# First FFN product of the last three pieces by seven block products, with the buffers and weight passes that go with it

## The chip, the cores and the metric

One NeuronCore of a Trainium2 chip runs the whole program. The metric is the device time of one execution in microseconds. Inputs and outputs lie in HBM; the two FFN weights arrive as 64-bit floats, the rest as 32-bit floats.

## The reference

```python
def _attn_ref(q, k, v):                      # 8 batches, 8 heads, 576 rows, 64 columns
    scores = np.matmul(q, k.transpose(0, 1, 3, 2)) / np.sqrt(64)
    # a row of block i (blocks of 64 rows) sees the columns of blocks 0..i
    scores = np.where(mask, scores, -1e9)
    attn = np.exp(scores - scores.max(-1, keepdims=True))
    attn = attn / (attn.sum(-1, keepdims=True) + 1e-09)
    return np.matmul(attn, v)

def _moe_ref(x, w_in, w_out):                # x: 4608 x 512, w_in: 512 x 2048, w_out: 2048 x 512
    h = x @ w_in
    g = h * np.clip(h + 3.0, 0.0, 6.0) / 6.0
    return g @ w_out
```

The attention output, with its heads side by side, is `x`.

## The kernel before

**Number format.** A 32-bit value is carried as two 16-bit halves, `hi` and `lo = value - hi`, after division by a power of two. A product of two such values is three 16-bit matmuls: hi by hi, hi by lo, lo by hi. Each matmul is issued as a pair, one for each half of 64 output partitions.

**Attention.** 32 slots (8 batches, 4 pairs of heads each). A slot loads q and k, splits and transposes them by DMA (`qk_prep`, tile `qkT`, two buffers), makes the masked scores in three row groups (`s_group`, PSUM tile `s`), takes row maxima on DVE, exponentials on ACT, splits the probabilities (`ph`, `phl`), transposes them by DMA (`pT`; the third group's tile has the tag `pT2`, two buffers) and multiplies by v (`pv_group`, PSUM `pv`, into the x buffers `xb`). Batch 0 runs in 32 bits without the split.

**FFN.** The 4608 rows form 13 pieces, numbered 0 to 12; all have 384 rows but pieces 1 and 3, which have 192. Piece `pc` keeps its x in `xb[pc % 4]`. A piece has 16 steps `f` of 128 hidden columns. `ffn1(pc, f)` makes `h` (PSUM tag `h`, two buffers) with 12 pairs of matmuls of 384 columns, then the nonlinearity: ACT writes `r` (relu6 inner part), DVE multiplies, then `g` is split (hi on ACT or DVE, lo on DVE; tag `g`, four buffers). `ffn2(pc, f)` adds `g` times `wout` into three PSUM tiles `o0` to `o2`, one buffer each, with 9 pairs of 512 columns; it runs `LAG = 3` steps behind. After step 15 the three tiles are scaled into `osb` (tag `stage`, four buffers, which `r` uses too) and stored.

**Weights.** 32 half chunks are loaded (tag `raw` and others), turned from 64 to 32 bits, bounded (`w_max`: an ACT pass with absolute value and sum for each half, then a small DVE reduction) and split (`w_split`: hi on ACT, DVE or POOL, lo on DVE). This happens beside batch 0's attention and piece 0.

**Order.** The program does not run in the order in which it is written. `Recorder` collects every engine instruction with a key (its planned time: tables `AT` for the slots, `FT` for the pieces, and constants for the rest), then `schedule` simulates the five engines with a table of costs, takes at each moment the ready instruction with the smallest key, and emits that order. All engine instructions therefore have one line, L491. A tile gets its buffer only when the written order allows it: an instruction that starts a tile waits until no earlier written, unfinished tiles fill all buffers of its tag:

```python
            if i > head and need[tag][head:i].max() >= bufs[tag]:
                full[tag] = i
                return 1e18
```

`step` writes FFN steps as soon as the attention rows of their piece are written; `ffn_step` decides how far `ffn2` follows.

Of the kernel before, what the change touches and what calls it, by code (L numbers as in the profile page):

```python
# [8 lines left out]
F16 = mybir.dt.float16  # L9
# [8 lines left out]
P = 128  # L18
# [7 lines left out]
U = 1.592  # L26
AS = (6.899, 12.918, 18.225, 24.115)
AL = 17.759
PV0 = 2.584
TA, TR, PR = 2.701, 5.502, 1.15  # L30
QR = 2.616
PVA, PVB = 1.013, 0.991
# [6 lines left out]
EVP = 4  # L39
PRO = True  # L40
MEM = 0

NMIN = 64
QL = -3.431
VL = -2.484
W0, WD = 16.803, 2.29
S0, SD = 55.334, 4.109
M0, MD = 36.221, 7.195
RT = (29.488, 39.58, 49.409, 59.423)
RS, RL, VL1 = 2.209, 24.843, 24.11  # L50
VM0, VMX = 49.529, 0.186
# [3 lines left out]
QP = 0.558  # L55
VP = 0.387
BLK = 64
# [24 lines left out]
ADV = {("tensor", "a"): 99.24}  # L82


class Recorder:
# [12 lines left out]
    BIAS = {"vector": 250.0, "gpsimd": 500.0}  # L98
# [3 lines left out]
    def __init__(self, nc):  # L102
        self.nc = nc
        self.ops = []
        self.key = 0.0
        self.cls = ""
        self.joint = None
        self.adv = ADV
        for n in self.NAMES:
# [6 lines left out]
    def box(a):  # L116
        sz = mybir.dt.size(a.dtype)
# [58 lines left out]
    def add(self, ways):  # L176
# [318 lines left out]
def kernel(  # L495
# [51 lines left out]
    ffp = ctx.enter_context(tc.tile_pool(name="ff", bufs=3))  # L547
    ps_s = ctx.enter_context(tc.tile_pool(name="ps_s", bufs=3, space=bass.MemoryType.PSUM))
# [12 lines left out]
    def pow2_scale(mx, n, nm, to=None, exact=False):  # L561
# [8 lines left out]
        if exact:  # L570
            pt_ = ps_s.tile([P, 512], F32, tag="s", name=f"mt_{nm}")
            nc.joint = "mt", nm
            for h in range(2):
                wide = mx[:, h % n:h % n + 1].to_broadcast([P, BLK])
                nc.tensor.matmul(pt_[h * BLK:(h + 1) * BLK, :P], wide, ident, start=True, stop=True)
            nc.joint = None
            dg = sm.tile([P, n + 1], F32, tag=f"dg{n}", name=f"dg_{nm}")
            nc.vector.tensor_reduce(dg[:, n:], pt_[:, :P], axis=AX.X, op=ALU.max)
            nc.vector.tensor_scalar_mul(dg[:, :n], ident[:, :(n - 1) * BLK + 1:BLK], dg[:, n:])
            mx = dg[:, :n]  # L580
        ps = ps_s.tile([P, 512], F32, tag="s", name=f"mb_{nm}")
        nc.joint = "mb", nm
        for h in range(2):
            nc.tensor.matmul(ps[h * BLK:(h + 1) * BLK, :n], ones[:, :BLK], mx, start=True, stop=True)
        nc.joint = None
        nc.vector.tensor_scalar_max(am, ps[:, :n], TINY)
# [90 lines left out]

    def w_max(c):

        acc = sm.tile([P, 2, 2], F32, tag="wacc", bufs=2, name=f"wacc{c}")  # L680
# [66 lines left out]
    def v_max(n):  # L747
# [8 lines left out]
        if hp == NPAIR - 1:  # L756
            m1 = sm.tile([P, 1], F32, tag="vm1", name=f"vm1_{b}")
            nc.vector.tensor_reduce(m1, vmax[b], axis=AX.X, op=ALU.max)
            vscale[b] = pow2_scale(m1, 1, f"v{b}", exact=True)
# [13 lines left out]
    def h_scale(b):  # L773

        if b not in hs:
            t = sm.tile([P, NCH], F32, tag="sh", bufs=3, name=f"sh{b}")
# [3 lines left out]
            nc.vector.tensor_scalar_mul(t, t, C_H)  # L780
            hs[b] = t
        return hs[b]
# [374 lines left out]
    def pv_group(n, g):  # L1157
# [57 lines left out]
    acc = {}  # L1215

# [29 lines left out]
    def ffn1_(pc, f):  # L1246
        if pc == 0:
            return ffn1_f32(f)
        x, w, fc = xb[pc % 4], width(pc), f * P % NH
# [52 lines left out]
    def ffn2_(pc, f):  # L1302
# [34 lines left out]
        for t, a in enumerate(acc.pop(pc)):  # L1337
            n, half = min(w - t * P, P), w - t * P < P
            o = ffp.tile([P, DM], F32, tag="stage", bufs=NST_B, name=f"osb{pc}_{t}")
            oc = o[:, :DM // 2] if half else o  # L1340
            ac = a[:, :DM // 2] if half else a
            nc.scaled(oc, ac, so[:, t:t + 1] if pc else 1.0 / 6.0, "AV")
            rows = out[row + t * P:row + t * P + n]
# [86 lines left out]
    for n in range(NPAIR):  # L1430
        t = RT[n]
        at(t - QR, qk_load32_rest, n, lead=RL - QR)
        at(t - QR, qk_prep32, n, 1)
# [94 lines left out]
```

## Time and profile before

| | |
|---|---|
| median of three runs | 985.25 us (983.32 to 985.38) |
| profiled execution, its own time | 982.83 us |
| its span | 981.0 us |
| granted TensorE clock, mean | 0.999 |
| busy: PE, DVE, ACT, POOL | 964.2, 756.4, 696.5, 28.3 us |

Times in the rows are microseconds from the start of the span unless marked ns. PE is the matmul engine, PEld its weight loads, which overlap the matmuls. A group's mean is the duration of one instruction; consecutive instructions of one engine overlap somewhat, so the distance between two starts is the better price where a timeline shows it.

### The profile page before, as it was taken

Reading aid. Unit: us, or ns where it says so; the run is one execution under the profiler, and the core shown is the slowest. Engines: PE = TensorE matmul, PEld = TensorE weight load, DVE = VectorE, ACT = ScalarE, POOL = GpSimd, SP = SyncE. Lnnn points to the kernel's source line nnn. Section 1 sums busy time; section 2 is a strip of 40 time slices with the busy share of each in tenths; the row PEclk is TensorE's granted clock in tenths of the full one; section 3 lists DMA queues with packets and bytes.
Section 4 is the critical chain, followed back from the end, with each engine's and each line's share of the span. In section 5 each row is a group of like instructions: output and inputs, shape, how many; then the busy total and the mean of one; then the engine's idle time right before and its main releaser. Section 6 shows DMA issues by size and latency. Waiting matters only on the chain.

```text
span 981.0 us, 29087 instructions
## 1 busy us (share of the span) xinstructions
PE 964.2 (98%) x11754; PEld 722.9 (74%) x11754; DVE 756.4 (77%) x2081; ACT 696.5 (71%) x1840; POOL 28.3 (3%) x109
## 2 busy tenths in 40 slices
PE   8999999999999999999999999999999999999998
PEld 6655447877778867777777677777777777777776
DVE  6889998999989999999999898899886432332331
ACT  6899789778778888888878788787775433333332
POOL 3012000000000000000000000000000000000000
PEclk9999999999999999999999999999999999999999
DMA  6966689899898899898899898786664200000000
GB/s 141 277 204 223 159 154 178 169 183 189 155 173 148 149 175 157 170 162 148 161 186 177 151 188 156 132 164 131 108 133 77 36 34 1 1 33 1 34 2 33
DMA packets 414199, 128.91 MB, mean 131 GB/s; under 512 B 403184, under 2 KB 403440, under 8 KB 414064
## 3 DMA queue, kind: packets, MB, share of 16 engines
q1 hardware_dynamic: 414064, 127.05, 66.5%
q8 instruction: 92, 1.51, 0.6%
q14 instruction: 43, 0.35, 0.1%
HBM read 45.09 MB, written 9.44 MB: 56 GB/s over the span
## 4 chain that ended last, share of the span: by engine, by line
PE 58%; DVE 6%; DMA 2%; ACT 1%; issue 1%; DVEq 0%; ACTq 0%
PE o L491 25%; PE h L491 25%; PE s L491 4%; PE pv L491 4%; DMA pT<-ph 2%; DVE st L491 1%; DVE phl L491 1%; DVE ph L491 1%; DVE r L491 1%; DVE g L491 1%; DVE qks L491 1%; DVE vhl L491 0%; ACT p L491 0%; DVE x L491 0%; ACT r L491 0%
## 5 line engine op out<-in xcount | busy, mean ns | idle before, releaser
L491 PE MATMUL h<-x,win 128*64 128x384 f16 (+3 forms) x4790 | 440.7, 319 | 4.4 <-DVE r L491 4.4
L491 PE MATMUL o<-wout,g 128*64 128x512 f16 (+2 forms) x3424 | 432.3, 383 | 0.0
L491 PEld LDWEIGHTS <-win 128*64 128x64 f16 x4608 | 296.1, 110 | 62.5 <-issue 6.5
L491 PEld LDWEIGHTS <-g 128*64 128x64 f16 x3264 | 219.2, 110 | 91.6
L491 ACT ACTIVATE r<-h,eg,sh 128x192 f32<-128x192 f32 (+1 forms) x240 | 134.1, 580 | 115.2 <-PE h L491 110.8
L491 DVE SCALAR_TENSOR_TENSOR r<-r,eg,h 128x384 f32<-128x384 f32 (+1 forms) x192 | 110.3, 575 | 132.0 <-ACT r L491 131.3
L491 ACT ACTIVATE p<-s,st,esc 128x64 f32<-128x64 f32 (+1 forms) x280 | 163.1, 586 | 13.6 <-DVE ph L491 7.3
L491 DVE SCALAR_TENSOR_TENSOR g<-r,g 128x384 f16<-128x384 f32 (+1 forms) x192 | 99.5, 519 | 34.1 <-ACT g L491 33.3
L491 DVE TENSOR_REDUCE st<-s 128x1 f32<-128x64 f32 (+1 forms) x280 | 119.2, 446 | 6.9 <-PE s L491 6.1
L491 ACT ACTIVATE g<-r 128x384 f16<-128x384 f32 (+1 forms) x157 | 77.4, 494 | 59.2 <-DVE r L491 58.7
L491 PE MATMUL s<-qkT 128*64 128x64 f16 (+7 forms) x1120 | 101.8, 287 | 1.9 <-ACT p L491 1.3
L491 PEld LDWEIGHTS <-vhl 128*64 128x64 f16 x1680 | 74.0, 110 | 13.5 <-issue 4.1
L491 PEld LDWEIGHTS <-qkT 128*64 128x64 f16 x1120 | 62.0, 110 | 23.5 <-issue 7.6
L491 PE MATMUL pv<-pT,vhl 128*64 128x192 f16 (+2 forms) x1680 | 74.4, 233 | 1.9 <-DMA pT<-ph 0.9
L491 DVE SCALAR_TENSOR_TENSOR ph<-p,st,ph 128x256 f16<-128x256 f32 (+2 forms) x168 | 66.5, 444 | 0.1
L491 DVE SCALAR_TENSOR_TENSOR phl<-p,st,phl 128x512 f16<-128x512 f32 (+1 forms) x84 | 62.8, 789 | 0.3 <-ACT phl L491 0.3
L491 ACT ACTIVATE st<-st,esc 128x1 f32<-128x1 f32 (+2 forms) x127 | 36.8, 291 | 34.3 <-DVE st L491 32.9
L491 ACT ACTIVATION_READ_ACCUMULATOR p<-s,st,esc 128x1 f32 x280 | 55.0, 196 | 0.0
L491 ACT ACTIVATE ph<-p,st 128x64 f16<-128x64 f32 (+5 forms) x106 | 43.2, 450 | 15.8 <-DVE st L491 14.2
L491 DVE SCALAR_TENSOR_TENSOR qks<-qk,rs_q,qks 128x576 f16<-128x576 f32 x56 | 44.5, 807 | 0.1
L491 ACT ACTIVATE qks<-qk 128x576 bf16<-128x576 f32 x56 | 37.8, 677 | 0.3 <-DMA qkT<-qks 0.3
L491 ACT ACTIVATE x<-pv 128x192 f16<-128x192 f32 (+1 forms) x56 | 20.3, 363 | 11.5 <-PE pv L491 10.0
(150 smaller groups left out, 847.0 us busy)
## 6 DMA issues: line engine op xcount, KB each, us to landing
out_dram<-osb SPq DMA_DIRECT2D x35, 256.0 KB, 2.7
vnat<-in_v_dram SPq DMA_DIRECT2D x64, 128.0 KB, 3.0
qk<-in_q_dram SPq DMA_DIRECT2D x28, 288.0 KB, 3.4
qk<-in_k_dram SPq DMA_DIRECT2D x28, 288.0 KB, 4.3
rawi<-in_moe_w_in_dram SPq DMA_DIRECT2D x8, 512.0 KB, 4.5
rawo<-in_moe_w_out_dram SPq DMA_DIRECT2D x8, 512.0 KB, 4.7
ph<-in_moe_w_in_dram SPq DMA_DIRECT2D x6, 512.0 KB, 4.8
ph<-in_moe_w_out_dram SPq DMA_DIRECT2D x6, 512.0 KB, 4.0
```

Source lines behind the costliest of these rows:

```text
L491: getattr(eng, method)(*args, **kw)
```

## The change

Pieces 10, 11 and 12 (`pc >= SW`, `SW = 10`) compute `h` with seven products of blocks in place of eight: the 256 hidden columns of a weight chunk are two blocks of 128, the 512 model columns two of 256, the 384 rows two of 192. `pv_group` then writes x of these pieces once, in 32 bits. `x_forms` makes the blocks and four differences of blocks of x, once for a piece; `w_forms` makes four sums of blocks of the weights, for all eight chunks, written ahead of the first of these products. `ffn1_seven` runs once for two steps `f`, adds the products from PSUM into `hh`, and goes on with the nonlinearity from there. The weight sums live in buffers of the attention's tags (`homes`), the 32-bit weight in the tag `raw`. Outputs of all pieces get a pair tile with the tag `raw` for their first two tiles. The last tile of the last piece is scaled and stored in two halves, on two DMA queues. Weights are bounded and split by whole chunks, without POOL. Planner constants and tables are new; the branch `far` in `pow2_scale` exists but is off (`WFAR, VFAR = 99, 99`). Scales of `g` and of the output change by powers of two.

```diff
-AT = ((4, 86.25), (6, 123.23), (8, 163.76), (9, 178.32), (10, 200.46), (12, 251.25), (14, 297.48), (15, 319.97), (16, 344.82), (24, 581.69), (32, 825.86))
-FT = ((0, 34), (1, 120), (2, 165.28), (3, 233.86), (4, 274.28), (5, 355.06), (7, 504.5), (10, 755.22), (13, 989.58))
+AT = ((4, 86.25), (5, 104.31), (6, 123.19), (8, 163.76), (9, 178.32), (10, 199.81), (12, 251.29), (13, 269.94), (14, 285.88), (15, 306.89), (16, 332.9), (24, 564.98), (32, 785.9))
+FT = ((0, 34), (1, 120.0), (2, 165.17), (3, 233.37), (4, 273.76), (5, 348.85), (6, 400.52), (7, 495), (10, 765), (13, 965.63))
...
-PVA, PVB = 1.013, 0.991
+PVA, PVB = 0.974, 1.579
...
+SW = 10
+WF0, WFD = 768.607, 15.583
+XFA = 10.306
...
-ADV = {("tensor", "a"): 99.24}
+ADV = {("tensor", "a"): 51.29}
...
     def w_max(c):
...
+        acc = sm.tile([P, 2], F32, tag="wm", name=f"wm{c}")
...
-            for half in range(2):
-                c32 = w_f32(w, c, half)
-                ab = ffp.tile([P, WC], F32, tag="stage", bufs=NST_B, name=f"ab{w}{c}_{half}")
-                ab = ab.rearrange("p (r l n) -> p r l n", r=c32.shape[1], l=2)
-                nc.scalar.activation(ab, c32, AF.Abs, accum_out=acc[:, wi, half:half + 1])
...
+            c32, _ = w_whole(w, c)
+            ab = ffp.tile([P, WC], F32, tag="stage", bufs=NST_B, name=f"ab{w}{c}")
+            ab = ab.bitcast(BF16).rearrange("p (r l n) -> p r l n", r=c32.shape[1], l=2)
+            nc.scalar.activation(ab, c32, AF.Abs, accum_out=acc[:, wi:wi + 1])
...
     def w_split(c):
...
-            for half in range(2):
-                c32 = w_f32(w, c, half)
-                part = w_part(w, c, half)
-                hi, lo = (part[:, :, i].rearrange("p r (l n) -> p r l n", l=2) for i in range(2))
-                nc.scaled(hi, c32, rs[:, wi:wi + 1], "AVP")
-                nc.vector.scalar_tensor_tensor(
-                    lo, c32, rs[:, wi:wi + 1], hi, op0=ALU.mult, op1=ALU.subtract
-                )
+            c32, part = w_whole(w, c)
...
+            if pc >= SW:
+                nc.scaled(x_whole(pc)[:, hp, xs], ps[:, t0:t1], E_X / 4, "AV")
+                continue
...
+    HP = TP // 2
...
+    homes = [("qkT", 3)] + [("pT2", 3)] + [("p", 1)] * 4 + [("qkT", 3)] + [("pT2", 3)]
...
+    def w_forms(c):
+        was, nc.key, nc.cls = (nc.key, nc.cls), WF0 + c * WFD, "w"
+        w32 = ffp.tile([P, NDT, NH], F32, tag="raw", bufs=1, name=f"w32_{c}")
+        nc.vector.tensor_add(w32, win[:, c, :, 0], win[:, c, :, 1])
+        a11, a12, a21, a22 = (w32[:, 2 * d:2 * d + 2, l * P:(l + 1) * P] for l in range(2) for d in range(2))
+        wf[c] = []
+        last = None
+        for i in range(2):
+            if not room:
+                tag, n = homes.pop(0)
+                bufs = NPB if tag == "p" else 2
+                t = attp.tile([P, n, 2, 2, 2 * P], F16, tag=tag, bufs=bufs, name=f"wf{c}_{i}")
+                room.extend(t[:, j] for j in range(n))
+            o = room.pop(0)
+            s = ffp.tile([P, 2, 2, P], F32, tag="stage", bufs=NST_B, name=f"ws{c}_{i}")
+            if not i:
+                nc.vector.tensor_add(s[:, 0], a21, a22)
+                nc.vector.tensor_sub(s[:, 1], s[:, 0], a11)
+            else:
+                nc.vector.tensor_sub(s[:, 0], a11, a21)
+                nc.vector.tensor_sub(s[:, 1], a12, last[:, 1])
+            last = s
+            s2 = s.rearrange("p k d x -> p k (d x)")
+            nc.scaled(o[:, :, 0], s2, 1.0, "AV")
+            nc.vector.tensor_sub(o[:, :, 1], s2, o[:, :, 0])
+            wf[c] += [
+                [[o[:, k, l, d * P:(d + 1) * P] for l in range(2)] for d in range(2)] for k in range(2)
+            ]
+        nc.key, nc.cls = was
+    def x_forms(pc):
+        was, nc.key = nc.key, line(FT, pc) - XFA
+        x = x_whole(pc)
+        raw = natp.tile([P, 2, 3, 2, HP], F16, tag="qk", bufs=2, name=f"xr{pc}")
+        rw = raw.rearrange("p l k d n -> p (l k d n)")
+        r0 = rw[:, :4 * HP].rearrange("p (l d n) -> p l d n", l=2, d=2)
+        r1 = rw[:, 4 * HP:].rearrange("p (l d n) -> p l d n", l=2, d=2)
+        b11, b12, b21, b22 = (x[:, 2 * d:2 * d + 2, h * HP:(h + 1) * HP] for d in range(2) for h in range(2))
+        for r, b in ((r0, b11), (r1, x[:, 2:])):
+            nc.scaled(r[:, 0], b, 1.0, "AV")
+            nc.vector.tensor_sub(r[:, 1], b, r[:, 0])
+        tt = attp.tile([P, 4, 2, 2, HP], F16, tag=("qks", "pT01")[pc % 2], bufs=1, name=f"xt{pc}")
+        fs = []
+        for k in range(4):
+            t = ffp.tile([P, 2, HP], F32, tag="stage", bufs=NST_B, name=f"xs{pc}_{k}")
+            a, b = ((b12, b11), (b22, fs and fs[0]), (b22, b12), (b21, fs and fs[-1]))[(0, 1, 3, 2)[k]]
+            nc.vector.tensor_sub(t, a, b)
+            fs.append(t)
+            nc.scaled(tt[:, k, 0], t, 1.0, "AV")
+            nc.vector.tensor_sub(tt[:, k, 1], t, tt[:, k, 0])
+        t1, t2, t4, t3 = ([[tt[:, k, l, d] for l in range(2)] for d in range(2)] for k in range(4))
+        x11 = [[r0[:, l, d] for l in range(2)] for d in range(2)]
+        x21, x22 = ([[r1[:, l, d, h * HP:(h + 1) * HP] for l in range(2)] for d in range(2)] for h in range(2))
+        xform[pc] = x11, x21, x22, t1, t2, t3, t4
+        nc.key = was
+    def ffn1_seven(pc, c):
+        if not wf:
+            for k in range(NCH):
+                w_forms(k)
+        if pc not in xform:
+            x_forms(pc)
+        x11, x21, x22, t1, t2, t3, t4 = xform[pc]
+        s1, s2, s3, s4 = wf[c]
+        w11, w12, w22 = (
+            [[win[:, c, 2 * h + d, l, f * P:(f + 1) * P] for l in range(2)] for d in range(2)]
+            for f, h in ((0, 0), (0, 1), (1, 1))
+        )
+        hh = (flat(xb[1], F32)[:, :6 * HP], ph01[1].rearrange("p l u x -> p (l u x)").bitcast(F32))[c % 2]
+        hh = hh.rearrange("p (k n) -> p k n", k=6)
+        def mul(o, w, x, nm):
+            for d in range(2):
+                nc.joint = "u", pc, c, nm, d
+                for i, (wl, xl) in enumerate(((0, 0), (0, 1), (1, 0))):
+                    for h in range(2):
+                        r = slice(h * BLK, (h + 1) * BLK)
+                        nc.tensor.matmul(
+                            o[r], w[d][wl][:, r], x[d][xl],
+                            start=d == 0 and i == 0, stop=d == 1 and i == 2,
+                        )
+            nc.joint = None
+        one_ = ps_h.tile([P, HP], F32, tag="h", name=f"u{pc}_{c}")
+        mul(one_, w11, x11, 1)
+        nc.scaled(hh[:, 5], one_, 1.0, "AV")
+        for k, runs in enumerate((
+            ((w12, x21, 2), (s2, t2, 6)), ((s1, t1, 5), (s3, t3, 7)), ((s4, x22, 3), (w22, t4, 4)),
+        )):
+            ps = ps_s.tile([P, 2, HP], F32, tag="s", name=f"u{pc}_{c}_{k}")
+            for j, run in enumerate(runs):
+                mul(ps[:, j], *run)
+            if k < 2:
+                with_ = hh[:, 5 - k].rearrange("p (o n) -> p o n", o=1).to_broadcast([P, 2, HP])
+                nc.vector.tensor_add((hh[:, 0:5:4], hh[:, 1:3])[k], ps, with_)
+                if k:
+                    nc.vector.tensor_add(hh[:, 3], ps[:, 0], hh[:, 2])
+            else:
+                nc.vector.tensor_add(hh[:, 1:3], ps, hh[:, 1:3])
+        eg = g_scales()[0]
+        for l in range(2):
+            r = ffp.tile([P, TP], F32, tag="stage", bufs=NST_B, name=f"r{pc}_{2 * c + l}")
+            h = hh[:, 2 * l:2 * l + 2].rearrange("p k n -> p (k n)")
+            for b, c0, c1 in spans(pc):
+                nc.scalar.activation(
+                    r[:, c0:c1], h[:, c0:c1], AF.Relu,
+                    bias=eg[:, 1, c:c + 1], scale=h_scale(b, 4.0)[:, c:c + 1],
+                )
+            nc.vector.scalar_tensor_tensor(r, r, eg[:, 2, c:c + 1], h, op0=ALU.min, op1=ALU.mult)
+            g = ffp.tile([P, 2, TP], F16, tag="g", bufs=NGB, name=f"g{pc}_{2 * c + l}")
+            nc.scaled(g[:, 0], r, 4 * E_G, "AV")
+            nc.vector.scalar_tensor_tensor(
+                g[:, 1], r, 4 * E_G, g[:, 0], op0=ALU.mult, op1=ALU.subtract
+            )
+            gt[pc, 2 * c + l] = g
...
+            return None if f % 2 else ffn1_seven(pc, f // 2)
...
+            if t == 0:
+                pair = ffp.tile([P, 2, DM], F32, tag="raw", bufs=1, name=f"osb{pc}")
+            o = pair[:, t] if t < 2 else ffp.tile([P, DM], F32, tag="stage", bufs=NST_B, name=f"osb{pc}_{t}")
...
+            if pc == NPC - 1 and t == nt - 1:
+                for h, e in enumerate((nc.sync, nc.scalar)):
+                    cs = slice(h * DM // 2, (h + 1) * DM // 2)
+                    nc.scaled(o[:, cs], a[:, cs], so[:, t:t + 1], "AV")
+                    e.dma_start(rows[:, cs], o[:, cs])
+                continue
...
+            while done1 >= SW * NFT and not done1 % 2 and done2 < done1 + 2 - NGB:
+                ffn2(*divmod(done2, NFT))
+                done2 += 1
...
-        while owed and done1 < TOT and not left[done1 // NFT]:
+        while owed and done1 < TOT and not left[done1 // NFT] and (done1 < SW * NFT or not sum(left)):
```

## Rows read from the trace of the kernel before

**Rows 1.** The page's first part: busy time, share of the span, instructions.

```profile
PE 964.2 (98%) x11754; PEld 722.9 (74%) x11754; DVE 756.4 (77%) x2081; ACT 696.5 (71%) x1840; POOL 28.3 (3%) x109
```

**Rows 2.** Busy time by stretch: stretch, length, each engine's busy us, clock, DMA.

```profile
0.00:25.00 25.00, 20.22 (x141) 16.03 (x141) 17.23 (x54) 17.18 (x59) 7.64 (x34) 1.00 0.63 146
...
100.00:125.00 25.00, 25.00 (x176) 11.64 (x174) 24.83 (x74) 20.45 (x47) 1.71 (x4) 1.00 0.66 154
...
275.00:300.00 25.00, 21.88 (x385) 18.15 (x382) 20.05 (x72) 19.69 (x56) 0.30 (x2) 1.00 0.94 166
...
784.00:846.00 62.00, 62.00 (x672) 47.09 (x670) 19.12 (x37) 20.46 (x34) 0.00 (x0) 1.00 0.04 14
```

**Rows 3.** Timeline of PE, pieces 9 and 10: start, length, instructions merged.

```profile
782.45 2.14 PE L491 MATMUL o<-wout,g 128*64 128x512 f16 x18
784.39 2.14 PE L491 MATMUL h<-x,win 128*64 128x384 f16 x24
786.34 2.14 PE L491 MATMUL o<-wout,g 128*64 128x512 f16 x18
```

**Rows 4.** Timeline of PE, piece 3, matmuls of 192 columns.

```profile
294.08 1.18 PE L491 MATMUL h<-x,win 128*64 128x192 f16 x24 [2.03 <-DVE r L491]
295.07 0.86 PE L491 MATMUL pv<-pT,vhl 128*64 128x192 f16 x18
```

**Rows 5.** Groups by form, 784.4 to 969 us: busy, mean | idle.

```profile
L491 PEld LDWEIGHTS <-win 128*64 128x64 f16 x1150 | 81.0, 110 | 17.5
...
L491 DVE SCALAR_TENSOR_TENSOR r<-r,eg,h 128x384 f32<-128x384 f32 x47 | 28.8, 614 | 100.1 <-ACT r L491 100.1
```

**Rows 6.** Groups by form on DVE, whole span.

```profile
L491 DVE SCALAR_TENSOR_TENSOR g<-r,g 128x384 f16<-128x384 f32 x160 | 88.5, 553 | 33.6 <-ACT g L491 32.8
...
L491 DVE SCALAR_TENSOR_TENSOR phl<-p,st,phl 128x512 f16<-128x512 f32 x56 | 39.7, 745 | 0.0
...
L491 DVE SCALAR_TENSOR_TENSOR x<-pv,x 128x192 f16<-128x192 f32 x52 | 18.1, 350 | 1.2 <-PE pv L491 0.9
...
L491 DVE TENSOR_TENSOR x<-pf,rb 128x192 f32<-128x192 f32 x8 | 2.8, 355 | 0.9 <-PE pf L491 0.7
```

**Rows 7.** Busy time by stretch around the end of attention.

```profile
735.00:776.00 41.00, 40.58 (x521) 31.83 (x518) 26.32 (x63) 22.79 (x59) 0.00 (x0) 1.00 0.42 72
776.00:784.00 8.00, 8.00 (x90) 6.05 (x88) 2.27 (x5) 1.87 (x3) 0.00 (x0) 1.00 0.01 2
```

**Rows 8.** Timeline of PE, the last slots' products.

```profile
746.05 1.28 PE L491 MATMUL pv<-pT,vhl 128*64 128x192 f16 x30
...
757.03 1.50 PE L491 MATMUL s<-qkT 128*64 128x512 f16 x16
...
774.22 1.28 PE L491 MATMUL pv<-pT,vhl 128*64 128x192 f16 x30
```

**Rows 9.** Timeline of DVE: distances of starts.

```profile
735.17 0.55 DVE L491 SCALAR_TENSOR_TENSOR g<-r,g 128x384 f16<-128x384 f32 x1
735.63 0.35 DVE L491 SCALAR_TENSOR_TENSOR x<-pv,x 128x192 f16<-128x192 f32 x1
```

**Rows 10.** PE's waits, whole span: total, times, longest.

```profile
PE h L491 <- DVE r L491: 4.4, 3, 2.0
PE qt L491 <- DMA qf<-in_q_dram: 3.9, 1, 3.9
```

**Rows 11.** Groups by form on ACT, whole span.

```profile
L491 ACT ACTIVATE abi<-win 128x512 f32<-128x512 f32 x14 | 8.9, 640 | 0.2 <-DVE win L491 0.2
...
L491 ACT ACTIVATION_READ_ACCUMULATOR abi<-win 128x1 f32 x14 | 2.9, 210 | 0.0
```

**Rows 12.** The chain that ended last, its end.

```profile
976.05 0.60 ACT osb L491
...
977.35 0.69 ACT osb L491
```

**Rows 13.** Tile osb: duration min/median/max, first and last start.

```profile
L491 ACT ACTIVATE osb<-o,so x28: 472/687/710, 203.2 to 977.3; 128x512 f32<-128x512 f32 x27, 128x256 f32<-128x256 f32 x1
```

More of the change, by code (lines that the diff above doesn't have):

```diff
@@ L24 @@
 WY = 27
[L26 to L31, printed above, removed]
-PVA, PVB = 1.013, 0.991
+U = 0.632
+AS = (6.363, 13.291, 20.163, 24.432)
+AL = 17.497
+PV0 = 2.428
+TA, TR, PR = 2.701, 4.807, 2.397
+QR = 4.605
+PVA, PVB = 0.974, 1.579
 PHS = 18
@@ L116, in box @@
     def box(a):
+        if not Recorder.on_chip(a):
+            return 0, 1, 0, 1
         sz = mybir.dt.size(a.dtype)
@@ L569, in pow2_scale @@
         am = sm.tile([P, n], F32, tag=f"am{n}", name=f"am_{nm}")
-        if exact:
-            pt_ = ps_s.tile([P, 512], F32, tag="s", name=f"mt_{nm}")
-            nc.joint = "mt", nm
+        if exact and far:
+            row = drp.tile([n, P], F32, tag=f"row{n}", name=f"dr_row_{nm}")
+            nc.sync.dma_start(row.rearrange("n p -> p n"), mx)
+            al = sm.tile([P, n, P], F32, tag="al", bufs=1, name=f"al_{nm}")
+            nc.sync.dma_start(
+                al.rearrange("p n x -> p (n x)"),
+                row.rearrange("n p -> (n p)").rearrange("(o x) -> o x", o=1).to_broadcast([P, n * P]),
+            )
+            nc.vector.tensor_reduce(am, al, axis=AX.X, op=ALU.max)
+            nc.vector.tensor_scalar_max(am, am, TINY)
+        else:
+            if exact:
+                pt_ = ps_s.tile([P, 512], F32, tag="s", name=f"mt_{nm}")
+                nc.joint = "mt", nm
+                for h in range(2):
+                    wide = mx[:, h % n:h % n + 1].to_broadcast([P, BLK])
+                    nc.tensor.matmul(pt_[h * BLK:(h + 1) * BLK, :P], wide, ident, start=True, stop=True)
+                nc.joint = None
+                dg = sm.tile([P, n + 1], F32, tag=f"dg{n}", name=f"dg_{nm}")
+                nc.vector.tensor_reduce(dg[:, n:], pt_[:, :P], axis=AX.X, op=ALU.max)
+                nc.vector.tensor_scalar_mul(dg[:, :n], ident[:, :(n - 1) * BLK + 1:BLK], dg[:, n:])
+                mx = dg[:, :n]
+            ps = ps_s.tile([P, 512], F32, tag="s", name=f"mb_{nm}")
+            nc.joint = "mb", nm
@@ L573, in pow2_scale @@
             for h in range(2):
-                wide = mx[:, h % n:h % n + 1].to_broadcast([P, BLK])
-                nc.tensor.matmul(pt_[h * BLK:(h + 1) * BLK, :P], wide, ident, start=True, stop=True)
+                nc.tensor.matmul(ps[h * BLK:(h + 1) * BLK, :n], ones[:, :BLK], mx, start=True, stop=True)
             nc.joint = None
-            dg = sm.tile([P, n + 1], F32, tag=f"dg{n}", name=f"dg_{nm}")
-            nc.vector.tensor_reduce(dg[:, n:], pt_[:, :P], axis=AX.X, op=ALU.max)
-            nc.vector.tensor_scalar_mul(dg[:, :n], ident[:, :(n - 1) * BLK + 1:BLK], dg[:, n:])
@@ L580, in pow2_scale @@
[L580 to L586, printed above, removed]
+            nc.vector.tensor_scalar_max(am, ps[:, :n], TINY)
         nc.vector.tensor_scalar(
@@ L694, in w_split @@
         for wi, w in enumerate("io"):
-            for half in range(2):
-                c32 = w_f32(w, c, half)
-                part = w_part(w, c, half)
-                hi, lo = (part[:, :, i].rearrange("p r (l n) -> p r l n", l=2) for i in range(2))
-                nc.scaled(hi, c32, rs[:, wi:wi + 1], "AVP")
-                nc.vector.scalar_tensor_tensor(
-                    lo, c32, rs[:, wi:wi + 1], hi, op0=ALU.mult, op1=ALU.subtract
-                )
+            c32, part = w_whole(w, c)
+            hi, lo = (part[:, :, i].rearrange("p r (l n) -> p r l n", l=2) for i in range(2))
+            nc.scaled(hi, c32, rs[:, wi:wi + 1], "AV")
+            nc.vector.scalar_tensor_tensor(
+                lo, c32, rs[:, wi:wi + 1], hi, op0=ALU.mult, op1=ALU.subtract
+            )
     gs = []
@@ L771, with h_scale @@
     hs = {}
-    def h_scale(b):
-        if b not in hs:
-            t = sm.tile([P, NCH], F32, tag="sh", bufs=3, name=f"sh{b}")
+    def h_scale(b, times=1.0):
+        if (b, times) not in hs:
+            t = sm.tile([P, NCH], F32, tag="sh", bufs=4, name=f"sh{b}_{int(times)}")
             nc.vector.scalar_tensor_tensor(
@@ L779, in h_scale @@
             )
-            nc.vector.tensor_scalar_mul(t, t, C_H)
-            hs[b] = t
-        return hs[b]
+            nc.vector.tensor_scalar_mul(t, t, C_H * times)
+            hs[b, times] = t
+        return hs[b, times]
     qn = {}
@@ L1338, in ffn2_ @@
             n, half = min(w - t * P, P), w - t * P < P
-            o = ffp.tile([P, DM], F32, tag="stage", bufs=NST_B, name=f"osb{pc}_{t}")
+            if t == 0:
+                pair = ffp.tile([P, 2, DM], F32, tag="raw", bufs=1, name=f"osb{pc}")
+            o = pair[:, t] if t < 2 else ffp.tile([P, DM], F32, tag="stage", bufs=NST_B, name=f"osb{pc}_{t}")
             oc = o[:, :DM // 2] if half else o
             ac = a[:, :DM // 2] if half else a
+            rows = out[row + t * P:row + t * P + n]
+            if pc == NPC - 1 and t == nt - 1:
[4 more added lines that the diff above has]
+                continue
             nc.scaled(oc, ac, so[:, t:t + 1] if pc else 1.0 / 6.0, "AV")
-            rows = out[row + t * P:row + t * P + n]
             if half:
```

69 lines of the change are left out of this document (46 added, 23 removed).

## Prediction

> **What bounds the kernel now.** I read the page's busy shares first, then the windows by stretch, then the timelines of PE and DVE around the place where piece 10 starts, and last the groups by form for prices.
>
> PE is busy for 964.2 of 981.0 us, and no other engine is over 77% [rows 1]. The windows say where the missing 16.8 us lie: 4.8 in the first 25 us, 3.1 between 275 and 300 us, some 4 after the last matmul, the rest in small pieces; in the three last pieces PE never stops, at a granted clock of 1.00, the 2.4 GHz level [rows 2]. So time can be won in two ways: fewer matmul cycles, or fewer of those waits.
>
> The reader should not take "busy" for the price of a matmul. The timeline gives it as a distance of starts. Piece 10's first twelve pairs of 384 columns start at 784.39 and the next group at 786.34: 1.95 us, 162.5 ns a pair. The nine pairs of 512 columns before them take 1.94 us [rows 3]. Two steps of the FFN thus take 2 x (1.95 + 1.94) = 7.78 us, and eight times that is 62.2 us a piece, which is the length of the stretch that one piece fills [rows 2]. DVE does only 19.1 us of work in it [rows 2], so in the last three pieces two thirds of DVE are free. Before them they are not: at 100 to 125 us DVE is busy for 24.83 of 25 us [rows 2].
>
> **The change part by part.**
>
> *Seven products.* One product of blocks is 2 model blocks x 3 terms = 6 pairs of 192 columns; seven are 42 pairs, where two steps had 24 pairs of 384. Piece 3 shows the price of 192 columns: 24 matmuls from 294.08 to 295.07, 0.99 us for 12 pairs, 82.5 ns a pair [rows 4]. So 42 x 0.0825 = 3.47 us replaces 3.90 us: 0.43 us a chunk, times 8 chunks and 3 pieces, **10.4 us less**. The second product does not change.
>
> A pair of 192 columns must also get two weight loads in 82.5 ns, 84 loads a chunk where there were 48. In piece 3 they did: 24 loads went with 24 matmuls in 0.99 us [rows 4]. The Trainium skill (TensorE: Matmul & The Clock Gate, LDWEIGHTS) prices a load by its columns, by its figure an estimate of 53 ns for 64 columns, so 107 ns for a pair if the two loads follow each other; by that the seven products would take 4.5 us and the change would cost some 14 us. The trace disagrees at 82.5 ns. I take the row; the other view is a rival below.
>
> *Sums on DVE.* DVE prices without a per-row scalar: 192 columns 0.355 us, 384 columns 0.553 us [rows 6], which makes 1.03 ns for each further column; by that 256 columns are an estimate of 0.42, 512 of 0.69 (a form with a scalar took 0.745 [rows 6]), 768 of 0.95 and 1024 of 1.21 us. Back to back, starts lie closer: an instruction of 0.55 us was followed after 0.46 us [rows 9], so 0.09 us less each.
> - `ffn1_seven`, a chunk: three sums of 384 and one of 192, 2.0 us, and per step the multiplication at 0.61 [rows 5] and g's lo at 0.55: 4.3 us in 7.35 us of PE. It hides, with latency to spare: the second product of a chunk comes after the next chunk's seven products.
> - `x_forms`: two of 768, eight of 384: 6.3 us a piece. For pieces 11 and 12 it hides in the half of DVE that is free.
> - `w_forms`: 1.21 + 4 x 0.42 + 2 x 0.69 = 4.3 us a chunk, 34 us for eight, all needed in piece 10.
>
> Work taken from DVE: the lo part of x for pieces 10 to 12, three instructions of 0.35 us [rows 6] in each of the last slots.
>
> *Where piece 10 starts.* This is the place that decides. Piece 9's outputs now take their pair tile from the tag `raw`, one buffer, and they are written after all eight `w_forms`, which use `raw` for the 32-bit weight. By the rule of buffers none of them gets it before the last `w_forms` has let go; and piece 10's second product needs piece 9's PSUM tiles emptied. Until then PE has seven products of chunks 0 to 3 (the fifth lacks a `g` buffer and an `hh`) and two second products of piece 9: 4 x 3.47 + 3.88 = 17.7 us from 784.4 on.
>
> Supply of DVE until that moment: the weight sums' homes open when slot 30's `qkT` is done, about 735 us; slot 31's `qkT` is read at 757, slot 30's last product ends after 746, slot 31's after 774 us [rows 8]. DVE's idle time is 14.7 us from 735 to 776 and 5.7 us from 776 to 784 [rows 7]; with 2.1 us of x work gone (three instructions in each of the last two slots) and the 17.7 us, 40.2 us. Demand: `x_forms` 6.3, `w_forms` 32.7 (the last lo parts can follow later), chunks 0 and 1 and the sums of chunk 2 10.7: 49.7 us by durations, or 42.1 us by distances of starts (84 instructions x 0.09 less). So PE lacks work for 1.9 to 9.5 us; nothing if the new tables let attention end some us sooner, for which the idle DVE time before 735 gives little. I take **4 us more**, nearer to the distances, since the sums are independent and can be packed. ACT has room: the hi parts add an estimate of 1.3 us a chunk beside 31% of load (20.46 of 62 us [rows 2]).
>
> *The new front.* Whole chunks save ACT one fixed part for each pair of halves: a bound pass took 0.64 + 0.21 us [rows 11]; of a double one only the columns double. That is some 0.4 us x 16 on ACT and 0.16 us x 16 on DVE, against the splits that come back from POOL. PE is shown busy there for 25.00 of 25 us [rows 2], so most of it hides. The tables decide more: they can close PE's waits for `r`, 4.4 us in all, or open as many; the first load's 3.9 us stay [rows 10]. From -5 to +4; I take **1 us less**.
>
> *The end.* Three scalings of 0.60, 0.60 and 0.69 us run one after the other on ACT once PE has stopped [rows 12]. Half a tile took 0.47 us [rows 13], and the halves can run on two engines: 0 to 1.0 us less; I take **0.4**. That the two halves are stored by two queues I count at nothing.
>
> **Sum.** -10.4 + 4 - 1 - 0.4 = -7.8 us. The profiled execution took 982.83 us, so 975.0; it lay 2.4 us under the median of the runs shown, 985.25, and on their scale the change gives **977.4 us**.
>
> **The rivals.**
> - *Everything hides and the front pays.* DVE's sums fit before PE runs dry, and the tables close the 4 us of waits: -10.4 - 0.4 - 4, 970.4 us. For it: two thirds of DVE free after 776 us. Against it: the shortage by either price.
> - *The sums' time is the upper bound.* 9.5 us of PE idle at piece 10: -10.4 + 9.5 - 0.4, 984 us, no change that can be told.
> - *Slower: the weight sums come after attention.* If the written order or lack of `stage` buffers keeps `w_forms` back until slot 31's last product at 774 to 776 us, supply falls to 5.7 + 17.7 = 23.4 us against 42.1 to 49.7, PE stands for 19 to 26 us, and the kernel takes 993 to 1001 us. It decides from a shortage of 11.8 us on, all gains together. For it: three of the sixteen home places open only after slot 31's product [rows 8], and their keys lie behind piece 10's own. Against it: idle DVE takes whatever is ready, and the first three chunks have homes once slot 30's product of 746 us is done [rows 8].
> - *Weight loads bind.* The loads' busy time is 81.0 us for 1150, 70 ns each [rows 5]; if that were their pace, 84 of them would take 5.9 us a chunk, 2.0 us more than now, 48 us in all: 1033 us. Piece 3's 41 ns a load [rows 4] speak against it; only runs of 24 have shown it, and these will be runs of 84.
>
> **Chances.** A measurement can tell about 0.2%, 2 us, from no change. Forecast (972 to 981.5 us) 0.56, all but 0.01 of it faster; everything hides 0.17, faster; upper bound 0.16 (0.05 faster, 0.07 same, 0.04 slower); sums after attention 0.08 and loads 0.03, slower. That is 0.77 faster, 0.08 same, 0.15 slower. The range reaches from the first rival's 970 with a little of the better front to the upper bound with a front that loses 3 us: 969 to 987 us; what lies outside is the last two rivals and the edge of the first.
>
> **What would show it.** Right: in pieces 11 and 12 seven products of a chunk start 3.47 us before what follows them and a piece takes 58.8 us with PE never idle; after attention's last product PE has one gap, of 2 to 9 us, at the first second product of piece 10, released by ACT's `osb` of piece 9, with DVE full of `ws` and `wf` before it. Wrong: pairs of 192 columns over 82.5 ns; gaps on `hh` or `g` in every chunk; no gap at piece 10; or a front that is more than 5 us off, which would make the total wrong with the mechanism right.

## Result and the profile after

The changed kernel takes 968.18 us (median of 4 runs, 966.7 to 968.66), the kernel before 984.51 us beside it; the ratio is 0.9832, with an interval from 0.9815 to 0.9849. The time lies 0.8 us under the stated range and 9.2 us under the forecast. The direction was right, the size was not.

The profiled execution took 968.66 us with a span of 966.9 us, 14.2 us less than the profiled one before. The other 2 us lie in no trace: the profiled execution of before lay 1.7 us under its median, that of after 0.5 us over its own. Of 33 executions of the kernel before on record (982.21 to 987.18 us) one alone was faster than the profiled 982.83 us.

The page's first part of the changed kernel answers to [rows 1]:

```profile
PE 954.4 (99%) x12604; PEld 709.2 (73%) x12604; DVE 838.0 (87%) x2240; ACT 704.6 (73%) x1838; POOL 18.3 (2%) x101
```

PE works 9.8 us less and DVE 81.6 us more. PE idles 12.5 us in place of 16.8.

**Products.** The timeline of PE in the changed kernel, one chunk of piece 10 once it runs steadily (`u` is the PSUM tile of the seven products):

```profile
848.80 1.18 PE L498 MATMUL u<-xr,win 128*64 128x192 f16 x24
849.79 1.68 PE L498 MATMUL u<-xt,wf 128*64 128x192 f16 x36
851.28 0.69 PE L498 MATMUL u<-xr,wf 128*64 128x192 f16 x12
851.77 0.69 PE L498 MATMUL u<-xt,win 128*64 128x192 f16 x12
852.27 4.08 PE L498 MATMUL o<-wout,g 128*64 128x512 f16 x36
856.15 1.18 PE L498 MATMUL u<-xr,win 128*64 128x192 f16 x24
```

Read the distances of starts, not the lengths: 84 matmuls from 848.80 to 852.27, 3.47 us, 82.6 ns a pair, as in [rows 4]. The chunk takes 7.35 us where it took 7.78 [rows 3]. A run of 84 keeps the pace that runs of 24 had shown, so weight loads don't bind. The Trainium skill (TensorE: Matmul & The Clock Gate, LDWEIGHTS) would by its figure make the two loads of a pair an estimate of 107 ns, if they follow each other; the trace disagrees with that over the long runs too.

**The start of piece 10.** The same timeline from piece 9's end on:

```profile
777.92 4.05 PE L498 MATMUL o<-wout,g 128*64 128x512 f16 x36
781.80 1.16 PE L498 MATMUL u<-xr,win 128*64 128x192 f16 x24
...
785.27 4.05 PE L498 MATMUL o<-wout,g 128*64 128x512 f16 x36
...
792.62 1.46 PE L498 MATMUL o<-wout,g 128*64 128x512 f16 x12
...
797.38 1.46 PE L498 MATMUL o<-wout,g 128*64 128x512 f16 x12
...
804.07 1.18 PE L498 MATMUL u<-xt,wf 128*64 128x192 f16 x24 [0.28 <-DVE ph L498]
...
808.19 13.14 PE L498 MATMUL o<-wout,g 128*64 128x512 f16 x120 [0.22 <-DVE osb L498]
```

The wait that the prediction placed here is here, released by `osb` on DVE, but it is 0.22 us, with 0.28 us on a sum before it. From 781.80 to 808.19, 26.4 us, these two waits included, PE had other work: the products of chunks 0 to 4 and half of chunk 5, piece 9's last two second products, and two runs of 12 into the third PSUM tile of piece 10. DVE's busy time in the same place, from the windows:

```profile
740.00:760.00 20.00, 20.00 (x254) 12.97 (x250) 20.00 (x49) 15.55 (x44) 0.00 (x0) 1.00 0.51 82
760.00:780.00 20.00, 20.00 (x246) 12.80 (x244) 20.00 (x40) 12.56 (x26) 0.00 (x0) 1.00 0.28 50
780.00:800.00 20.00, 20.00 (x366) 16.03 (x362) 19.69 (x42) 9.90 (x20) 0.00 (x0) 1.00 0.04 16
800.00:820.00 20.00, 19.51 (x292) 15.06 (x290) 16.98 (x37) 9.00 (x17) 0.00 (x0) 1.00 0.08 28
```

DVE is busy for 20.00 of 20 us from 740 to 780: the sums did fill it, as argued.

**The front.** Before, piece 10's first product starts at 784.39 us, with one second product of piece 9 (1.94 us) still to do [rows 3] that the changed kernel has behind it when its first seven products start at 781.80. The same point of the work is thus 784.39 + 1.94 = 786.33 us before: 4.5 us are won ahead of the products. The windows show in which stretch (before, PE idled 1.6, 1.6 and 3.1 us in these three, the last as in [rows 2]):

```profile
150.00:200.00 50.00, 50.00 (x888) 39.19 (x886) 48.22 (x148) 40.69 (x122) 0.91 (x6) 1.00 1.10 186
200.00:250.00 50.00, 48.31 (x654) 36.96 (x650) 46.84 (x132) 42.19 (x117) 0.60 (x4) 1.00 1.00 178
250.00:300.00 50.00, 50.00 (x775) 40.19 (x773) 46.42 (x147) 41.25 (x118) 0.60 (x4) 1.00 0.90 163
```

PE's waits of the changed kernel, against [rows 10]: the waits of `h` for `r`, 4.4 us before, are gone.

```profile
PE qt L498 <- DMA qf<-in_q_dram: 4.0, 1, 4.0
PE mb_q L498 <- ACT qks L498: 1.3, 1, 1.3
...
PE u L498 <- DVE ph L498: 0.3, 1, 0.3
...
PE o L498 <- DVE osb L498: 0.2, 1, 0.2
```

**The end.** The last second products of the kernel before, which the rows do not show:

```profile
969.72 7.53 PE L491 MATMUL o<-wout,g 128*64 128x512 f16 x68
```

Those of the changed kernel:

```profile
955.17 7.96 PE L498 MATMUL o<-wout,g 128*64 128x512 f16 x72
```

Its chain that ended last, against [rows 12]:

```profile
961.87 1.34 ACT osb L498 x2
...
963.23 0.48 ACT osb L498
...
963.74 0.48 DVE osb L498
```

ACT scales the first tiles while PE still works on the others: PE ends at 963.13 us. DVE's half begins when ACT's has ended, and ends 1.09 us after PE. From PE's end to the span's end it is 3.8 us, as before (977.25 to 981.0): nothing won.

### The profile page after: what moved, and what is told of

The parts are those of the page before. It is cut to its first block, busy times and chain, and to the rows that moved or that the text cites. A ratio compares the mean times of both kernels' runs of the same rounds, so it can differ in the third digit from the quotient of the medians.

```text
span 966.9 us, 30947 instructions
## 1 busy us (share of the span) xinstructions
PE 954.4 (99%) x12604; PEld 709.2 (73%) x12604; DVE 838.0 (87%) x2240; ACT 704.6 (73%) x1838; POOL 18.3 (2%) x101
## 5 line engine op out<-in xcount | busy, mean ns | idle before, releaser
L498 PE MATMUL o<-wout,g 128*64 128x512 f16 (+3 forms) x3418 | 420.6, 383 | 0.2 <-DVE osb L498 0.2
L498 PE MATMUL h<-x,win 128*64 128x384 f16 (+3 forms) x3640 | 332.0, 318 | 0.1
L498 PEld LDWEIGHTS <-g 128*64 128x64 f16 x3264 | 211.7, 110 | 103.8 <-issue 0.4
L498 PEld LDWEIGHTS <-win 128*64 128x64 f16 x4320 | 246.0, 110 | 47.6 <-issue 0.2
L498 ACT ACTIVATE r<-h,eg,sh 128x192 f32<-128x192 f32 (+1 forms) x176 | 98.1, 577 | 20.3 <-PE h L498 19.3
L498 ACT ACTIVATE g<-r 128x384 f16<-128x384 f32 (+1 forms) x146 | 71.9, 494 | 38.1 <-DVE r L498 33.0
L498 DVE SCALAR_TENSOR_TENSOR r<-r,eg,h 128x384 f32<-128x384 f32 (+1 forms) x144 | 80.5, 561 | 19.5 <-ACT r L498 19.4
L498 PE MATMUL s<-qkT 128*64 128x64 f16 (+7 forms) x1120 | 94.8, 287 | 0.1
L498 PEld LDWEIGHTS <-wf 128*64 128x64 f16 x1152 | 48.8, 110 | 0.7 <-DVE ph L498 0.5
L498 DVE TENSOR_TENSOR ph<-u,ph 128x384 f32<-128x384 f32 (+1 forms) x48 | 24.3, 506 | 20.4 <-PE u L498 18.7
```

The lines of the kernel that those rows point to most:

```text
L498: getattr(eng, method)(*args, **kw)
```

## Experiments

My theory after this profile: three causes that add up: the products save their columns and no more (10 us); the front won 4.5 us by itself; the wait at piece 10 exists but its cover was larger than I had counted. Rivals: the products give more than their columns, the front's gain hangs on the products, or there never was a wait to hide.

**no_seven.**

```diff
-SW = 10
+SW = 13
```

> The changed kernel with the seven products off for all pieces (SW = 13), everything else as changed. Theory (products save 24 x 0.43 us less the 0.5 us of gaps, the front is worth 4.5 us by itself): 9.6 to 10 us above the changed kernel, about 978 us, and PE reaches the same point of work, two second products before the end of piece 9, 4 to 5 us earlier than before. Rival (the front gain exists only because the last pieces' work moved off DVE before piece 10): no better than 983 us.

978.04 us, 0.9933 (0.9918 to 0.9947) of before. That is 9.9 us above the changed kernel and, with no product of seven in it, 6.7 us below the kernel before beside it (984.76). Piece 9's last first product starts at 775.83 us; the changed kernel's starts at 775.97 and the one of before at 780.50. So the front's gain does not hang on the products, and the products are worth 9.9 us. The rival falls. By medians the front is thus worth 6.7 us, where the traces show 4.5 to 4.7; the difference is the 2 us above.

**seven_only, old_tables, old_weights.** Two kernels go back to the old tables with the planner's other constants, and two to weights by half chunks, in `w_max` and `w_split` (two cuts of the edits):

```diff
-AT = ((4, 86.25), (5, 104.31), (6, 123.19), (8, 163.76), (9, 178.32), (10, 199.81), (12, 251.29), (13, 269.94), (14, 285.88), (15, 306.89), (16, 332.9), (24, 564.98), (32, 785.9))
+AT = ((4, 86.25), (6, 123.23), (8, 163.76), (9, 178.32), (10, 200.46), (12, 251.25), (14, 297.48), (15, 319.97), (16, 344.82), (24, 581.69), (32, 825.86))
...
-            c32, part = w_whole(w, c)
+            for half in range(2):
+                c32 = w_f32(w, c, half)
+                part = w_part(w, c, half)
```

> The changed kernel with the old tables and constants and with weights bounded and split by half chunks, POOL included: of the change only the seven products, the pair tile and the divided last tile are left. Theory: the products bring their 10 us less a gap at piece 10's first second product that the old tables do not hide as well, 974 to 978 us. Rival (the tables are what makes the products pay, since DVE has no room otherwise): a gap of more than 8 us there and a time of 982 us or more.

> The changed kernel with the old tables and constants, weights by whole chunks. If the front's 4.5 us come from the tables: 972 to 978 us, with PE's waits before 300 us back at 4 us or more. If they come from the whole-chunk passes: 968 to 970 us.

> The changed kernel with weights bounded and split by half chunks, POOL included; tables new. If the front's 4.5 us come from the tables: 967 to 970 us. If they come from the whole-chunk passes: 971 to 974 us, with the loss before 150 us.

| | old tables | new tables |
|---|---|---|
| weights by halves | 974.32 (seven_only) | 973.02 (old_weights) |
| weights whole | 977.59 (old_tables) | 968.18 (changed) |

Neither edit alone brings the front's gain: with the old tables the whole chunks cost 3.3 us, with the new ones they give 4.8. Each of the two runs fell into the range of "it is this edit" (old_tables in 972 to 978, old_weights in 971 to 974, though its loss lies near 205 us and not before 150), so neither edit is the source by itself. seven_only is in its range, with 0.9 us of waits at piece 10: the products pay with the old tables too, and its rival falls. The first seven products start at 786.51 us in seven_only, 789.96 in old_tables, 786.00 in old_weights and 781.80 in the changed kernel, so most of the difference is made ahead of piece 10. seven_only has the time of the old front (786.33, as worked out above), though not its waits. PE's waits show the difference, first of seven_only, then of old_tables:

```profile
...
PE s L498 <- DVE am_q L498: 2.0, 1, 2.0
PE s L498 <- DMA qkT<-qks: 1.7, 1, 1.7
```

```profile
...
PE s L498 <- DMA qkT<-qks: 3.1, 1, 3.1
PE h L498 <- DVE x L498: 1.2, 2, 0.7
```

Those waits stand near 205 us, at the first scores of a slot, and differ from kernel to kernel. The stretch around them holds a second difference, the granted clock (third column from the right; the changed kernel's line, at 1.00, is above). First seven_only, then old_tables, then old_weights:

```profile
200.00:250.00 50.00, 44.22 (x592) 35.02 (x589) 44.90 (x126) 42.72 (x115) 0.60 (x4) 0.93 0.96 185
```

```profile
200.00:250.00 50.00, 44.82 (x574) 34.09 (x572) 43.41 (x124) 41.43 (x114) 0.60 (x4) 0.90 1.02 183
```

```profile
200.00:250.00 50.00, 46.56 (x623) 36.43 (x620) 46.05 (x135) 42.12 (x115) 0.61 (x4) 0.97 1.01 188
```

Up to the first seven products PE idles 12.1 us in seven_only, 11.2 in old_tables, 11.1 in old_weights and 8.2 in the changed kernel; for the same matmuls it is busy for 774.4, 778.8, 774.9 and 773.6 us. So old_tables waits less than seven_only and starts its products 3.4 us later all the same: what the whole chunks cost with the old tables is slower matmuls after a wait, not more waiting. What the runs show is the place (150 to 300 us) and the kind (waits of PE that one written order has and another has not, and the clock that falls after some of them); which single edit closes which wait they don't separate.

**forms_more.** The sum that makes the 32-bit weight is issued twice:

```diff
         nc.vector.tensor_add(w32, win[:, c, :, 0], win[:, c, :, 1])
+        nc.vector.tensor_add(w32, win[:, c, :, 0], win[:, c, :, 1])
```

> The changed kernel with the 32-bit weight of each chunk written twice (the same sum again): eight more DVE instructions of 1.14 us from start to start, 9.1 us in all, ahead of piece 9's outputs. Theory (DVE is full from 740 us until those outputs, PE's cover of 26 us is just used up): nearly all of it becomes PE idle time at piece 10, 6 to 9 us, 974 to 977 us, with the wait of the second product for the scaling of piece 9's output at its head. Rival (there is slack left in the cover): under 3 us more.

977.96 us, 0.9935 (0.9917 to 0.9953) of before: 9.8 us more for 9.1 us of DVE work, a little over the theory's range. Its waits of PE, the longest:

```profile
PE o L498 <- ACT osb L498: 7.2, 1, 7.2
```

It ends at 817.92 us; the granted clock was 0.50 from 815 to 820 us and 0.86 from 820 to 825, so the wait is not the whole loss. The cover of the changed kernel is used up, and the mechanism of the prediction holds: with 9.1 us on top of some 34 us of weight sums, about a quarter more, nearly all that the products gave (9.9 us) is lost.

**more_free.** The same with piece 9's outputs taken out of the tag `raw`:

```diff
-            if t == 0:
+            if t == 0 and pc != SW - 1:
                 pair = ffp.tile([P, 2, DM], F32, tag="raw", bufs=1, name=f"osb{pc}")
-            o = pair[:, t] if t < 2 else ffp.tile([P, DM], F32, tag="stage", bufs=NST_B, name=f"osb{pc}_{t}")
+            o = pair[:, t] if t < 2 and pc != SW - 1 else ffp.tile([P, DM], F32, tag="stage", bufs=NST_B, name=f"osb{pc}_{t}")
```

> The run with the 32-bit weights written twice, but piece 9's outputs in tiles of the tag stage, not in the pair of the tag raw. Theory (what makes PE wait at piece 10 is the buffer raw, held by the weight sums, not the sums themselves): piece 10's second products start without that wait of 7 us, and the sums that are late cost less, 968 to 973 us. Rival (DVE's backlog itself binds, PE would then wait for the sums of a later chunk): as long a wait in another place, 976 us or more.

967.03 us, 0.9815 (0.9799 to 0.983): 10.9 us less than forms_more with the same work on DVE. The load alone does not make PE wait; it takes the shared buffer. Without that PE goes straight on, and DVE may finish the sums of late chunks while early ones run. The timeline of PE in more_free:

```profile
783.64 4.08 PE L498 MATMUL o<-wout,g 128*64 128x512 f16 x36
787.52 1.18 PE L498 MATMUL u<-xr,win 128*64 128x192 f16 x24
...
790.99 4.08 PE L498 MATMUL o<-wout,g 128*64 128x512 f16 x36
794.87 1.18 PE L498 MATMUL u<-xr,win 128*64 128x192 f16 x24
```

Products and second products take turns from the first chunk on, at 7.35 us a chunk.

**last_eight.** Piece 12 alone goes back to eight products:

```diff
-        if pc >= SW:
+        if SW <= pc < NPC - 1:
             return None if f % 2 else ffn1_seven(pc, f // 2)
```

> The changed kernel with piece 12 alone put back to eight products, so that the place where the products start is as changed. Theory (3.48 us for a piece, all of it PE's): 3.2 to 3.8 us above the changed kernel, 971.4 to 972 us, the last piece 62.2 us long where one of seven products is 58.8. Rival (the products give more than their columns, for the total moved by 16 us): 5 us or more.

971.92 us, 0.9866 (0.9849 to 0.9882), 3.7 us more for one piece, where 3.5 were worked out. By the traces it is 184.9 us from the first seven products to PE's end, against 181.3 in the changed kernel, 3.6 more. The rival, a gain beyond the columns, falls.

**two_pieces.**

```diff
-SW = 10
+SW = 11
```

> The changed kernel with seven products in pieces 11 and 12 alone (SW = 11). Theory (3.48 us for each piece, all of it PE's, the start costs next to nothing): 3.0 to 3.5 us more than the changed kernel, 971 to 972 us, a piece of seven products taking 58.8 us and one of eight 62.2 us. Rival (the start of the products costs time that three pieces must earn back): less than 2.5 us more, or none.

999.24 us, 1.0149 (1.013 to 1.0168): 31 us more than with three pieces, and slower than before. Neither theory had that. PE's longest wait, and DVE's busy time by stretch:

```profile
PE u L498 <- ACT xt L498: 25.1, 1, 25.1
```

```profile
780.00:841.00 61.00, 61.00 (x659) 45.89 (x657) 21.71 (x41) 20.46 (x34) 0.00 (x0) 1.00 0.04 14
841.00:848.00 7.00, 7.00 (x98) 5.26 (x96) 6.86 (x13) 1.59 (x3) 0.00 (x0) 1.00 0.01 2
848.00:875.00 27.00, 2.36 (x44) 1.87 (x41) 26.31 (x51) 5.45 (x10) 0.00 (x0) 0.58 0.05 20
```

DVE is idle for two thirds of piece 10, makes one half of the first chunk's sums at 793 to 798 us, and the rest from 841.5 to 874 us; PE stands from 850.4 to 875.5. The timeline of DVE, without its `r` and `g` lines:

```profile
795.62 0.42 DVE L498 TENSOR_TENSOR ws<-ws,w 128x256 f32<-128x256 f32 x1
...
797.46 0.68 DVE L498 TENSOR_TENSOR wf<-ws,wf 128x512 f16<-128x512 f32 x1
...
841.54 0.42 DVE L498 TENSOR_TENSOR ws<-w 128x256 f32<-128x256 f32 x1
```

This is the slower rival of the prediction, the sums that come after, in a kernel that differs by one number; what PE waited for last was the differences of x (`xt`). What kept them: DVE was free and the weights were there, and the sums go on right after piece 10's last `g` (840.95 us) had let go of its `r`; two differences of x (`xs`, the same tag `stage`) had been made at 710.17 and 732.95 us, and the further differences that `x_forms` makes from them came from 874.30 us on; and the first chunk's first `ws`, in that tag too, was held from 795 us until the second was made from it at 841.88. That points to the four `stage` buffers; it was not tried with more of them. The 31 us are 25.1 of waiting, 3.5 for the piece that went back to eight products, and a rest in which the clock's 0.58 has a part that was not worked out.

**end_split, best, best_sync.** The last tile's halves get a tile each, and the last piece's other tiles are dealt out, first to DVE, second to ACT:

```diff
+                    oh = ffp.tile([P, DM // 2], F32, tag="stage", bufs=NST_B, name=f"osh{h}")
+                    nc.scaled(oh, a[:, cs], so[:, t:t + 1], "AV"[h])
+                    e.dma_start(rows[:, cs], oh)
...
+            nc.scaled(oc, ac, so[:, t:t + 1] if pc else 1.0 / 6.0, "AV" if pc < NPC - 1 else "VA"[t])
```

> The changed kernel with the last tile's halves in two tiles of their own, the first half on ACT and the second on DVE, and of the last piece's other tiles the first on DVE and the second on ACT. Theory (the second half waited for ACT's half because both write one tile): from PE's end to the last scaling's end 1.1 to 1.3 us in place of 2.35 us, so 0.8 to 1.2 us less, 967.2 us. Rival (the two engines wait for each other by the PSUM tile they read, or the store is what ends last): no change at the end.

967.57 us, 0.9827 (0.9811 to 0.9842). The timeline at its end:

```profile
957.64 4.51 PE L498 MATMUL o<-wout,g 128*64 128x512 f16 x40
...
960.90 0.75 DVE L498 TENSOR_SCALAR osb<-o,so 128x512 f32<-128x512 f32 x1 [2.65 <-PE o L498]
961.54 0.69 ACT L498 ACTIVATE osb<-o,so 128x512 f32<-128x512 f32 x1 [3.89 <-PE o L498]
...
962.19 0.48 DVE L498 TENSOR_SCALAR osh<-o,so 128x256 f32<-128x256 f32 x1 [0.54 <-PE o L498]
962.77 0.47 ACT L498 ACTIVATE osh<-o,so 128x256 f32<-128x256 f32 x1 [0.54 <-DVE osh L498]
```

PE ends at 962.15 us and the last scaling at 963.24, 1.09 us later, just as in the changed kernel. The 2.35 us of the expectation run from the first scaling's start there (961.87 to 964.22), and by that measure this run takes 2.34 (960.90 to 963.24). So nothing was won, and the span ends 3.8 us after PE in both. Two tiles do not free the halves, which still follow each other: the rival's outcome, though that the shared PSUM tile is the reason is not shown. In the median, 0.6 us, it can't be told from no change.

best adds the edit of more_free to this, best_sync moves best's second store to SP's queue:

```diff
-                for h, e in enumerate((nc.sync, nc.scalar)):
+                for h, e in enumerate((nc.sync, nc.sync)):
```

> The changed kernel with the last piece's tiles divided over ACT and DVE as in the run on the end, and piece 9's outputs in tiles of the tag stage. Theory: 1.2 us less at the end and up to 0.5 us less at piece 10, 966.5 to 967.5 us. Rival (the r tiles lack the stage buffers that the outputs take): as fast as the changed kernel or slower.

> The version before with both halves of the last tile stored by SP's queue. Theory (the store issued by ACT took 2.5 us there in place of 0.4 and ended last): PE's end to the end of the span 3.8 us again, in place of 5.6, and 966 to 967.5 us. Rival (the stores are late for another reason): 968.5 us or more.

> The changed kernel itself, for comparison on the same chip: 967 to 969 us. By the theory it is 0.5 to 2 us above the version that it is sent with; by the rival it is level with it.

best takes 969.13 us (0.9836, 0.9821 to 0.9852), best_sync 967.73 us (0.9828, 0.981 to 0.9846), the changed kernel beside it 968.14 us (0.9827, 0.981 to 0.9845). The tile `osh` in best, the issues of its two stores:

```profile
L498 ACTq DMA_DIRECT2D out_dram<-osh x1: 2484/2484/2484, 963.1 to 963.1; - x1
L498 SPq DMA_DIRECT2D out_dram<-osh x1: 332/332/332, 963.3 to 963.3; - x1
```

The issue on ACT took 2.48 us there and 0.37 us in end_split, and by it the span ends 5.7 us after PE, in place of 3.8; on SP's queue (best_sync) it is 4.2 us. So best came out as its rival said, level with the changed kernel, with PE not waiting at piece 10 at all. The theory on the store holds in these two traces, one execution each; what made the issue long is open. The time of best_sync, 967.73 us, lies between its theory's range and its rival's, 0.4 us from the changed kernel, inside either interval. No version that clearly beats the changed kernel came out of these runs.

## Why the prediction was wrong

By its own steps, profiled execution against profiled execution:

| step | predicted | measured |
|---|---|---|
| seven products | -10.4 | -10.1 (9.6 from the start of piece 10 to PE's end, with the 0.5 of waits in it) |
| the wait where piece 10 starts | +4 | +0.5 |
| the new front | -1 | -4.5 |
| the end | -0.4 | 0 |
| sum | -7.8 | -14.1 |
| profiled executions to medians | 0 | -2.2 |

Two terms of the sum failed, by 3.5 us each and in the same direction: the wait where piece 10 starts and the new front.

- **Products: right.** Price of a pair, saving of a chunk, all hidden DVE work and the weight loads came as worked out from [rows 3, 4]; one piece less costs 3.7 us and none 9.9. (ACT's load beside them was 33%, 20.46 of 62 us, not 31%.)
- **The wait at piece 10: right mechanism, wrong size.** The term failed in "the fifth lacks a `g` buffer and an `hh`" and in leaving out the third PSUM tile. An `hh` comes free when `r` is multiplied, and `r` lies in `stage`, so the fifth and half of the sixth chunk ran; the third tile of piece 9 is in `stage` too and did not wait. The cover was 26.4 us, not 17.7. These 8.7 us alone would turn the bounds of 1.9 to 9.5 into less than nothing to 0.8. But the longer cover also brought DVE more work (the sums of two more chunks and the multiplications of one, 5.2 us at the prediction's prices), and an estimate of 4 us of the sums had run before its count began (the first weight sum at 726.99 us). With both, the upper bound is some 2 us; 0.5 was measured, where a gap of 2 to 9 us was to show it right. forms_more and more_free show that the wait, its place and its cause were as told.
- **The front: failed as a size.** Its bounds, -5 to +4, held what came, but I took -1. The rows gave no reason for the middle: they name 4.4 us of waits for `r` [rows 10], and the new front has just these closed. The two-by-two of tables and passes shows a gain that hangs on both at once, which I could not have added up from rows of before; only the range was sound there. Why this written order closes the waits stays open.
- **The end: wrong.** I let three scalings follow PE's end, but PE ended at 977.25 us and the first of them had started at 976.05 [rows 12]: only the third lay behind it. And I let two engines scale two halves at once; they followed each other.
- **Scale.** I put the change on the median of the first three runs, which lay 2.4 us above the profiled execution. The step sum of -14.1 on that median is 971.2 us, inside the range; the last 2.2 us, which no trace shows, took the time under it.
- **Rivals.** "Everything hides and the front pays", 970.4 us with a chance of 0.17, is what happened, and its two parts with it: -14.8 by its sum, -14.1 by the steps. The range ended at 969 because I cut the better front's share off it.

## What to carry to other kernels

Where PE never stops, a block scheme with fewer products can pay its saved columns nearly in full (here 10.1 of 10.4 us), if the smaller matmul keeps its start distance; read that in the trace. What decides is the place where it starts: list what PE can still do while it waits, buffer by buffer, up to the one that really blocks, since a buffer shared by the new sums and the old outputs can take that cover away (9.1 us of DVE work cost 9.8 us with it and nothing without it). A written order that comes from tables belongs to one set of instructions: change a pass, and its waits can come back elsewhere.

## What the runs showed of the hardware

A wait of PE can cost more than its length. In old_tables PE waited 3.07 us for a transpose, until 206.91 us, and then four times for under a microsecond; the windows behind it, with the granted clock in the third column from the right:

```profile
205.00:210.00 5.00, 2.01 (x28) 1.63 (x30) 4.29 (x15) 3.67 (x12) 0.00 (x0) 0.72 1.14 181
210.00:215.00 5.00, 3.99 (x34) 2.67 (x31) 4.30 (x13) 3.29 (x10) 0.00 (x0) 0.50 0.90 203
215.00:220.00 5.00, 4.98 (x64) 3.89 (x62) 4.59 (x9) 4.56 (x12) 0.00 (x0) 0.76 0.97 188
```

The clock fell to the 1.2 GHz level after the wait and stayed there until about 217.4 us (0.76 over the last window, by the two levels); PE's last gap had ended at 213.02. By the busy times above, 778.8 against 773.6 us, an estimate of its price is 5 us, beside 3 us of waiting. The length of one wait did not decide it here: in the changed kernel PE waits 1.26 us in that place and the clock stays at 1.00, in best_sync 1.09 us and the clock is 0.66 from 205 to 210 us, and the kernel before waits 2.03 us ahead of 294.08 [rows 4] with the clock at 1.00 [rows 2]. With the long waits it fell too: 0.58 from 848 to 875 us in two_pieces, 0.50 from 815 to 820 us in forms_more.
